# In-place transposed exponentials, a V product in three parts, early pair inputs and late weight sums in a fused attention and MLP kernel

## The chip, the cores and the metric

The kernel runs on one core of one Trainium2 chip. The metric is the device time of one execution in microseconds. The five engines work at once, each through its own instructions in order: PE (TensorE) multiplies matrices into PSUM, DVE (VectorE) and POOL (GpSimd) work element by element, ACT (ScalarE) applies functions and rounds, SP (SyncE) issues the transfers. Data lies in SBUF (128 partitions), sums of products in PSUM, the rest in device memory.

## What is computed

Attention with rotary positions over 4 batches of 8 heads, 576 tokens, 64 per head; its output, with the heads side by side, goes through a layer norm and a two-layer MLP with a residual sum. The weights are given in float64.

```python
scores = scale * np.matmul(q_rot, k_rot.transpose(0, 1, 3, 2))
scores = scores - np.max(scores, axis=-1, keepdims=True)
attn = np.exp(scores)
attn = attn / (np.sum(attn, axis=-1, keepdims=True) + 1e-09)
x = np.matmul(attn, v)                            # then (4, 576, 512)
xn = (x - mu) / np.sqrt(var + 1e-06) * g_ln
ch = np.maximum(xn @ w_ch1, 0.0) @ w_ch2          # 512 -> 2048 -> 512
return (x + ch).astype(np.float32)
```

## The kernel before

**First part.** The 32 heads are done as 16 head pairs, one after another (`attention(i)`). For each, PE makes scores in nine units of 128 by 576 (L430, the last one L426), each in one of four PSUM slots `sc` of two banks. DVE takes the maximum of each unit (L465), ACT the exponential with its row sums (L475), into a tile `p` (ring of two, each for two units; `p9` for the ninth). DVE transposes each unit in blocks of 32 from `p` into `pt` (L491, L488), of which there is one buffer for all nine units. When all nine are turned, PE multiplies them with V (`pv`, L539: 144 products of float32, 288 in the trace since each takes two passes) into two `sc` slots, DVE scales the result into `xt` (L555, L559) with inverse sums that went through memory (`write` L510, `read` L517 and L518). POOL rotates Q and K (L389, L391).

Between these lies other work: 32 weight tiles are decoded from float64 to float32 (`decode`, DVE L702 and L708, POOL L705, ACT L696 and L699) and split into a rounded high part and a low rest (`high` L721, `low` L725); the first 512 tokens (block 0) are normalised and go through the MLP as 32 units of 12 products (`mlp_unit`, L820). `weight_sums` makes, for each of eight stages (y, g), four sums of quarters of the weights (`tt` L771), splits them (L778, L781) and writes them to memory (L794) for the second part. A task of kind `how = {"POOL": 1.3, "DVE": 0.68}` goes to whichever of the two engines the planner finds free.

**Second part.** The other four blocks of 448 tokens are done as two pairs of blocks with a Strassen-like scheme: per pair eight stages of seven products of 12 matmuls (L973), with weights loaded from memory into a ring `w` of six buffers (`load_w`, L743 for the sums, L746 for plain quarters). `pair_inputs` makes the operands `x` of a pair: it loads four tiles of the normalised blocks for c = 0 into the one buffer `xc` of ring `ln` (L930), takes differences on POOL or DVE (L918), rounds on ACT and takes low parts (L900, L907), and then does the same for c = 1. The loads of the first pair wait for `late1`, that is, for all decoding, all weight sums and nearly all of block 0's MLP; the products of the second part use PSUM and SBUF that attention gives back (`late`, `switch`).

**Order.** Each piece of work is a task with a duration, dependencies, rings it takes from and gives to, and a priority. `Plan.run` runs the program once in its own time and records the tasks in the order in which they start there; that order is fixed on every engine. Priorities come from nominal times.

Of the kernel before, what the change touches and what calls it, by code (L numbers as in the profile page):

```python
# [10 lines left out]
F32 = mybir.dt.float32  # L11
# [9 lines left out]
P = 128  # L21
S = 576
# [19 lines left out]
RINGS = {"sc": 4, "m": 0, "p": 2, "p9": 1, "pt": 1, "x": 2, "xs": 3, "v": 1, "inv": 2, "w64": 2, "fw": 2, "w": 6, "h": 4, "xn": 1, "ln": 1, "sq": 1, "xt": 5, "n": 0, "o": 0, "tmp": 0, "ws": 2}  # L42
NPLAIN = 1
WP = 448
LATE = {"n": 6, "o": 13, "tmp": 9}
# [12 lines left out]
SLACK = 0.7  # L58
XPRIO = 1e4
XB = 0.0  # L60
WARM = 16
HOLD = {28: (14, 2), 29: (15, 0), 30: (15, 2), 31: (15, 4)}
ORDERED = True
ORDER = []
SIZES = 0.5, 2.0, 5.0, 12.0, 30.0
SHARE = 0.08, 0.01, 0.1, 0.3, 0.3
# [4 lines left out]
def mixed(x):  # L71
    for m in (0x7FEB352D, 0x846CA68B):
        x = ((x ^ x >> (16 if m == 0x7FEB352D else 15)) * m) & 0xFFFFFFFF
    return x ^ x >> 16


def chance(seed, i):
    return mixed((mixed(seed) + i * 0x9E3779B9) & 0xFFFFFFFF) / 2.0**32


def reorder(tasks):
    kinds = {}
    kind = [kinds.setdefault(t.fn.__code__, len(kinds)) for t in tasks]
    n = len(tasks)
    for seed in ORDER:
        m = mixed(seed)
        size, mode, later = SIZES[m % 5], m // 5 % 5, m // 25 % 5 == 0
        lo = int(chance(seed, 7) * n) if mode == 3 else 0
        for i in range(lo, min(lo + 60, n) if mode == 3 else n):
            t = tasks[i]  # L90
            if later and "SP" not in t.how:
                continue
            k = kind[i] + 1000003 if mode in (0, 4) else i
            if chance(seed, 2 * k + 100) < SHARE[mode]:
                d = size * (2 * chance(seed, 2 * k + 101) - 1)
                if later:
                    t.release += d
                else:
                    t.prio += d
# [10 lines left out]
class Plan:  # L110
# [32 lines left out]
    def run(self):  # L143
# [6 lines left out]
        while waiting:  # L150
            later = []
            started = False
            for t in waiting:
# [23 lines left out]
                e = min(t.how, key=lambda e: (begin(e), t.how[e]))  # L177
# [33 lines left out]
def rope_attention_then_ln_mlp(  # L211
# [32 lines left out]
    ap, xp, vpool, pp, ptp, smp = passing("attn"), passing("x", RINGS["x"]), passing("v", RINGS["v"]), passing("p", RINGS["p"]), passing("pt"), passing("small", 4)  # L244
# [27 lines left out]
    sums_w = {(y, g, i): dp.tile([P, 2, NC * P], F32, name=f"s{y}{g}{i}") for y in range(2) for g in range(4) for i in (3, 5, 6, 7)}  # L272
    split_w = {u: dp.tile([P, 2, NC * P], F32, name=f"v{u}") for u in UNITS}
# [158 lines left out]
    def attention(i):  # L432
# [3 lines left out]
        for c in range(5):  # L436
# [15 lines left out]
            ts = add({"PE": 0.6 if halved else 1.15 if c < 4 else 0.97}, go, need, N, take=["sc"] * len(units), give=["xk", "xq"] if c == 4 else [], lag=0.2, release=N - 2 if slow else 0, name=f"s{i}.{c}", behind=attention_order[-1:])  # L452
# [7 lines left out]
            for j, n in enumerate(units):  # L460
# [6 lines left out]
                def e(c=c, j=j, n=n):  # L467
                    if c == 4:
                        p = st["p", i, c] = pp.tile([P, S], F32, name="p9", bufs=1)
                    else:  # L470
                        if j == 0:
                            st["p", i, c] = pp.tile([P, 2, S], F32, name="p")
# [5 lines left out]
                take = ["p9"] if n == 8 else ["p"] if j == 0 else []  # L478
# [3 lines left out]
        for c in range(5):  # L482
            def turn(c=c):
                if ("pt", i) not in st:
                    st["pt", i] = ptp.tile([P, 9, S], F32, name="pt")
                pt, p = st["pt", i], st.pop(("p", i, c))
                if c == 4:
                    DVE.transpose(pt[:, 4], p)  # L488
                    return
# [5 lines left out]
            turned.append(add({"DVE": 0.68 if c == 4 else 1.36}, turn, need + turned[:1], N, take=["pt"] if c == 0 else [], give=["p9"] if c == 4 else ["p"], name=f"t{i}.{c}"))  # L495
# [30 lines left out]
        def pv():  # L526
            pt, v = st.pop(("pt", i)), st["v", i]
            st["pv", i] = tiles = [banks[k] for k in plan.task.got["sc"]]
            for b in range(18):
# [34 lines left out]
        t = add({"PE": 5.2}, pv, turned + [ev["v", i]], N, take=["sc", "sc"], give=["pt", "v"], lag=0.2, name=f"pv{i}")  # L564
        found = pieces(b)
        for piece in found:
# [10 lines left out]
            x = add({"DVE": dur}, go, [t, rd], N, behind=[] if fresh else [ev["fresh", n]], take=["xt"] if fresh else [], give=["sc", "sc", "inv"] if piece == found[-1] else [], of=t)  # L577
# [96 lines left out]
    def decode(k):  # L674
# [42 lines left out]
        t5 = add({"DVE": 0.68}, d2, [t4], prio, give=["w64"], port=True)  # L717
# [41 lines left out]
    def weight_sums(y, g):  # L759
# [3 lines left out]
        z, made = {}, {}  # L763

        def view(n):
            r, c = divmod(n, 2)
            f = st["fw", b].bitcast(F32).rearrange("p (r h) (c n) -> p r h c n", r=2, c=2)
            return f[:, r, :, c, :]
# [7 lines left out]
        def high(n):  # L776
            z[n] = wsp.tile([P, 2, NC * P], F32R, name="ws")
            ACT.copy(part(n, 0), view(n))  # L778
# [4 lines left out]
        how = {"POOL": 1.3, "DVE": 0.68}  # L783
        l = [t for k in range(k0, k0 + NC) for t in ev["wr", k]]
# [5 lines left out]
        for i, n, s in ((5, 3, s1), (7, 2, s3), (6, 0, s2), (3, 1, s4)):  # L790
            h = add({"ACT": 0.62}, lambda n=n: high(n), [s], prio, take=["ws"], behind=ev.get("sh", []))
            ev["sh"] = [h]
            read.append(add(how, lambda n=n: low(n), [h], prio, port=True))
            done.append(add({"SP": 512 / RATE}, lambda i=i, n=n: SP.dma_start(sums_w[y, g, i], raw(z[n])), read[-1:], prio, give=["ws"]))  # L794
        add({"NONE": 0.0}, lambda: None, read, prio, give=["fw"])
        ev["sums", (y, g)] = add({"NONE": 0.0}, lambda: None, done, prio)


    def mlp_unit(k, prev):
# [6 lines left out]
        dur = max(0.115, 0.008 + 0.43e-3 * W)  # L806
# [23 lines left out]
        if n and y % 8 != 4 and y:  # L830

            a = t = add({"PE": 12 * dur}, lambda: (group(0), group(1)), need + rest + ev["wr", k], prio, behind=ahead, take=["sc"], give=give, lag=0.2, name=f"m{k}")
        else:
            a = add({"PE": 6 * dur}, lambda: group(0), need + ev["wr", k], prio, behind=ahead, take=["sc"], name=f"m{k}")
            t = add({"PE": 6 * dur}, lambda: group(1), [a] + rest, prio + 0.5, give=give, lag=0.2)
# [43 lines left out]
    def switch():  # L879
        early.close()  # L880
        for name, n in LATE.items():
            kw = {"space": PSUM} if name == "n" else {}
            late[name] = ctx.enter_context(tc.tile_pool(name="late_" + name, bufs=n, reuse_waits="tile", **kw))
        late["acc"] = ctx.enter_context(tc.tile_pool(name="late_acc", bufs=1, reuse_waits="tile"))
# [313 lines left out]
```

## Time and profile before

| | |
|---|---|
| median of 3 runs | 766.96 us (765.75 to 774.95) |
| profiled execution | 771.92 us, its span 770.1 us |
| last V product ends | 452.2 us |
| PE busy, all | 648.7 us (84%) |
| DVE busy, all | 559.1 us (73%) |
| POOL, ACT busy, all | 439.1 us, 320.5 us |
| granted PE clock, mean | 0.902 |

Times in rows are microseconds from the start of the span, durations of one instruction ns. An engine's busy time is what its instructions cover; a row that gives a wait says how long the engine was idle before an instruction and what ended that.

### The profile page before, as it was taken

How to read it: one execution, taken by the hardware profiler on the slowest of the kernel's cores; microseconds unless marked ns; L12 is line 12 of the kernel's file. 1: busy time of each engine (PE TensorE's matmuls, PEld its weight loads, DVE VectorE, ACT ScalarE, POOL GpSimd, SP SyncE). 2: the span in 40 equal slices, each digit the busy share in tenths (PEclk: the TensorE clock that was granted, in tenths of full speed). 3: DMA queues.
4: the chain of work that ended last, by engine and by line, in shares of the span. 5: the costliest groups of instructions: out<-in, count | busy, mean ns of one | idle time of the engine just before them, and what ended most of it. 6: DMA issues, size and time to landing. Idle time of an engine off the chain costs nothing.

```text
span 770.1 us, 17931 instructions
## 1 busy us (share of the span) xinstructions
PE 648.7 (84%) x7218; PEld 512.7 (67%) x7218; DVE 559.1 (73%) x900; ACT 320.5 (42%) x662; POOL 439.1 (57%) x335
## 2 busy tenths in 40 slices
PE   6587677999878887877778644999999799999997
PEld 5464355676555564654556434788999699999997
DVE  5687876987778887786788435787676848757574
ACT  2355336625538356345555213534243305332230
POOL 3745765576677568687675015184166944544163
PEclk8878977899799998997999686999999899999999
DMA  9467775658796887767789632575876587666664
GB/s 263 128 192 200 187 216 193 180 151 265 175 269 219 261 246 273 193 210 256 204 253 307 205 106 76 176 254 184 292 214 220 190 261 250 213 219 215 218 201 145
DMA packets 92611, 163.33 MB, mean 212 GB/s; under 512 B 12144, under 2 KB 57712, under 8 KB 92528
## 3 DMA queue, kind: packets, MB, share of 16 engines
q1 hardware_dynamic: 91392, 161.33, 68.1%
q8 instruction: 57, 0.93, 0.5%
q10 hardware_dynamic: 1136, 0.85, 0.4%
q14 instruction: 26, 0.21, 0.1%
HBM read 124.32 MB, written 37.82 MB: 211 GB/s over the span
## 4 chain that ended last, share of the span: by engine, by line
PE 68%; DVE 15%; issue 5%; DMA 4%; ACT 4%; SPq 2%; POOL 1%; DVEq 0%; ACTq 0%; POOLq 0%
PE n L973 35%; PE sc L539 12%; PE sc L820 11%; PE sc L430 6%; DVE pt L491 5%; DVE mx L465 4%; ACT p L475 3%; PE sc L426 2%; DMA inv<-sums 2%; PE sc L617 1%; DMA xc<-hat 1%; POOL xc L918 1%; DVE xc L624 1%; DVE xt L555 1%; DVE fw L708 1%
## 5 line engine op out<-in xcount | busy, mean ns | idle before, releaser
L973 PE MATMUL n<-x,w 128*128 128x448 f32 x672 | 145.8, 375 | 17.8 <-ACT x L900 16.9
L475 ACT ACTIVATE p<-sc,mx 128x576 f32<-128x576 f32 x144 | 105.5, 738 | 126.7 <-DVE mx L465 119.4
L973 PEld LDWEIGHTS n<-x,w 128*128 128x128 f32 x672 | 127.9, 192 | 33.1 <-ACT x L900 18.2
L430 PE MATMUL sc<-xk,xq 64*128 64x288 f32 x512 | 109.2, 502 | 33.5 <-ACT p L475 20.7
L973 PE MATMUL n<-o,w 128*128 128x448 f32 x576 | 123.2, 372 | 4.6 <-DVE o L907 3.3
L539 PE MATMUL sc<-pt,v 32*64 32x160 f32 (+1 forms) x4608 | 100.5, 312 | 30.5 <-issue 24.1
L491 DVE STREAM_TRANSPOSE pt<-p 128x576 f32<-128x576 f32 x128 | 91.2, 752 | 41.7 <-PE sc L539 40.9
L973 PEld LDWEIGHTS n<-o,w 128*128 128x128 f32 x576 | 109.4, 191 | 16.3 <-DVE o L907 3.6
L539 PEld LDWEIGHTS sc<-pt,v 32*64 32x64 f32 x4608 | 89.0, 140 | 43.8 <-issue 29.1
L465 DVE TENSOR_REDUCE mx<-sc 128x1 f32<-128x576 f32 x144 | 101.3, 741 | 15.5 <-PE sc L430 13.3
L430 PEld LDWEIGHTS sc<-xk,xq 64*128 64x128 f32 x512 | 63.2, 219 | 71.7 <-ACT p L475 32.0
L900 ACT ACTIVATE o<-tmp 128x448 fp32r<-128x448 f32 x96 | 55.1, 578 | 100.4 <-PE n L973 46.0
L907 POOL TENSOR_TENSOR o<-tmp,o 128x448 fp32r<-128x448 f32 x57 | 72.4, 1298 | 25.2 <-ACT o L900 25.2
L1045 DVE TENSOR_TENSOR xt<-xt,n 128x448 f32<-128x448 f32 x80 | 49.0, 617 | 26.6 <-PE n L973 26.4
L725 POOL TENSOR_TENSOR w<-fw,w 128x512 fp32r<-128x512 f32 x26 | 33.2, 1280 | 56.1 <-ACT w L721 47.8
L705 POOL TENSOR_TENSOR fw<-fw,w 128x512 int32<-128x512 int32 x32 | 42.2, 1323 | 34.1 <-DVE fw L702 15.2
L820 PE MATMUL sc<-hh,w 128*128 128x512 f32 x128 | 49.5, 448 | 9.9 <-ACT p L475 9.9
L820 PE MATMUL sc<-xh,w 128*128 128x512 f32 x128 | 49.3, 452 | 5.7 <-ACT p L475 5.7
L1032 POOL TENSOR_TENSOR tmp<-tmp 128x448 f32<-128x448 f32 x16 | 21.4, 1336 | 55.3 <-DVE tmp L1011 55.3
L391 POOL TENSOR_TENSOR xs<-xs,rope_sb 128x576 f32<-128x576 f32 x30 | 46.7, 1556 | 0.5 <-DMA xs<-in_qk 0.5
L918 POOL TENSOR_TENSOR xc<-xc 128x448 f32<-128x448 f32 x16 | 21.4, 1334 | 41.8 <-DMA xc<-hat 38.3
L1011 DVE SCALAR_TENSOR_TENSOR tmp<-tmp 128x448 f32<-128x448 f32 x48 | 42.8, 912 | 0.2
(101 smaller groups left out, 972.7 us busy)
## 6 DMA issues: line engine op xcount, KB each, us to landing
w<-s SPq DMA_DIRECT2D x64, 512.0 KB
w<-v SPq DMA_DIRECT2D x96, 256.0 KB
v<-in_vp SPq DMA_DIRECT2D x64, 320.0 KB
s<-ws SPq DMA_DIRECT2D x32, 512.0 KB
xs<-in_qk SPq DMA_DIRECT2D x30, 288.0 KB
w<-in_w1p SPq DMA_DIRECT2D x16, 512.0 KB
v<-w SPq DMA_DIRECT2D x16, 512.0 KB
w<-in_w2p SPq DMA_DIRECT2D x16, 512.0 KB
```

Of the source, the lines that this page charges most:

```text
L391: eng().tensor_tensor(out=x[step], in0=x[step], in1=rope_sb[:, step], op=ALU.mult)
L430: PE.matmul(ps[:, a, :HS], lhsT=q[r, c * P : (c + 1) * P], rhs=k[r, KEYS[a]], start=True, stop=True)
L465: DVE.tensor_reduce(out=mx, in_=st["ps", i, n][:, :, :HS], axis=AX.XY, op=ALU.max, negate=True)
L475: ACT.activation(out=halves(p), in_=st.pop(("ps", i, n))[:, :, :HS], func=AF.Exp, bias=st.pop(("mx", i, n)), scale=1.0, accum_out=total)
L491: DVE.transpose(pt[:, 5 * j + c], p[:, j])
L539: PE.matmul(tiles[a // 2][j * D : (j + 1) * D, a % 2, x0 : x0 + (u1 - u0) * BLK], lhsT=v[r, of, k * P + j * D : k * P + (j + 1) * D], rhs= ...
L820: PE.matmul(ps, lhsT=wt, rhs=x, start=c + m == 0, stop=c + m == NC + 1)
L900: ACT.activation(out=o[0], in_=x(), func=AF.Relu if relu else AF.Copy)
L907: eng().tensor_tensor(out=lo, in0=x(), in1=raw(hi), op=ALU.subtract)
L973: PE.matmul(ps, lhsT=wt, rhs=x, start=fresh and kc + z == 0, stop=kc + z == 3, skip_group_check=True)
L1011: return lambda: DVE.scalar_tensor_tensor(out=out(), in0=x(), scalar=0.0, in1=y(), op0=ALU.max, op1=ALU.subtract)
L1045: DVE.tensor_tensor(out=o, in0=o, in1=ps(which, h), op=ALU.add)
```

## The change

Seven edits:

1. Exponentials are written straight into `pt`, of which there are now two buffers, and turned there in place, two units with one instruction; the rings `p` and `p9` are gone.
2. The V product is three tasks of 48 products each, between which others can be put.
3. `pair_inputs` loads both halves at once, into `xc`, three buffers of `sq` and one of `acc`, without waiting for `late1`, and takes the operands of both halves in turn.
4. For g = 3, `weight_sums` writes only the whole decoded weights to memory (`whole_w`, 1 MB each); `late_sums` reads them back in the second part (ring `lf`), makes the sums on POOL alone and writes them.
5. Rings: `w` 6 to 4, `inv` 2 to 1, `ws` 2 to 1, `sq` 1 to 3.
6. Every task's priority is a number from a table, and its earliest time is zero.
7. Planner durations, a few per cent each.

```diff
-RINGS = {"sc": 4, "m": 0, "p": 2, "p9": 1, "pt": 1, ..., "inv": 2, ..., "w": 6, ..., "sq": 1, ..., "ws": 2}
+RINGS = {"sc": 4, "m": 0, "pt": 2, ..., "inv": 1, ..., "w": 4, ..., "sq": 3, ..., "ws": 1, "lf": 0, "ls": 0}
+LATE = {"n": 6, "o": 13, "tmp": 9, "lf": 1, "ls": 1}
+DEFERRED = 6
+PLACES = (
+    "AAAFAGAPAUAKAFAAAZA-A)A;A8A#A#ArAvAzBFA^BQA[BdAeAAAoA[A}BMBVBGBcBdAwB8B6B(BoB%B:B,B[B=CBCRCFCmB~CPCeBnB=CVC1CuCvC&C=DYC:DDDgD%D!AjB7B.B_BACo",
...
+    places = "".join(PLACES)
+    for t, hi, lo in zip(tasks, places[::2], places[1::2], strict=True) if places else ():
+        t.prio, t.release = 0.1 * (len(CODE) * CODE.index(hi) + CODE.index(lo)), 0.0
...
-                        p = st["p", i, c][:, j]
+                    if n == 0:
+                        st["pt", i] = ptp.tile([P, 9, S], F32, name="pt")
+                    p = st["pt", i][:, 5 * j + c]
...
-                for j in range(2):
-                    DVE.transpose(pt[:, 5 * j + c], p[:, j])
+                p = st["pt", i][:, 4] if c == 4 else st["pt", i][:, c::5]
+                DVE.transpose(p, p)
...
-            for b in range(18):
+            for b in range(6 * part, 6 * part + 6):
...
-        t = add({"PE": 5.2}, pv, turned + [ev["v", i]], N, take=["sc", "sc"], give=["pt", "v"], lag=0.2, name=f"pv{i}")
+        t0 = t = add({"PE": 1.75}, lambda: pv(0), turned + [ev["v", i]], N, take=["sc", "sc"], name=f"pv{i}")
+        t = add({"PE": 1.75}, lambda: pv(1), [t], N)
+        t = add({"PE": 1.75}, lambda: pv(2), [t], N, give=["pt", "v"], lag=0.2)
...
+        if b < DEFERRED:
+            read, ev["sums", (y, g)] = make_sums(y, g, lambda: st["fw", b].bitcast(F32), l, prio, wsp, "ws", {"POOL": 1.3, "DVE": 0.68})
+            add({"NONE": 0.0}, lambda: None, read, prio, give=["fw"])
+            return
+        t = add({"SP": 1024 / RATE}, lambda: SP.dma_start(whole_w[y, g], st["fw", b].bitcast(F32)), [ev["d2", k] for k in range(k0, k0 + NC)], prio)
...
+    def late_sums(y, g, prio):
+        def load():
+            st["lf", y, g] = late["lf"].tile([P, NC, NC * P], F32, name="lf")
+            SP.dma_start(st["lf", y, g], whole_w[y, g])
+
+        t = add({"SP": 1024 / RATE}, load, [ev["whole", (y, g)], ev["late"]], prio, take=["lf"], name=f"lf{y}{g}")
+        read, ev["sums", (y, g)] = make_sums(y, g, lambda: st["lf", y, g], [t], prio, None, "ls", {"POOL": 1.3})
...
+                    if c == 0:
+                        if s == 0:
+                            x["all"] = lnp.tile([P, NC, BLOCK], F32, name="xc")
+                        x[c, s] = x["all"][:, s, :WP]
+                    elif s == 1:
+                        x[c, s] = lnp.tile([P, BLOCK], F32, name="acc")[:, :WP]
+                    else:
+                        x[c, s] = lnp.tile([P, BLOCK], F32, name="sq", bufs=RINGS["sq"])[:, :WP]
...
+                last = l[c, s] = add({"SP": 224 / RATE}, load, hats_, prio - 20, take=take, behind=[last] if last else [], name=f"hl{q}.{c}.{s}")
```

The table moves nearly every task. Three places show what matters below.

The first is DVE at the seam of the second and third head pair (`sc` are PSUM slots; `total` and `row` belong to the sums of a head pair, 208 before and 207 now to the second). Before, the third pair's first transpose is the last row shown, behind all of the second pair's:

```order
L491 STREAM_TRANSPOSE pt<-p 128x576 x2
L488 STREAM_TRANSPOSE pt<-p_622 128x576
L503 RECIPROCAL total_208<-total_208 128x9
L505 STREAM_TRANSPOSE row<-total_208 128x32
L465 TENSOR_REDUCE mx<-sc_111 128x1
L465 TENSOR_REDUCE mx<-sc_113 128x1
L465 TENSOR_REDUCE mx<-sc_114 128x1
L708 SCALAR_TENSOR_TENSOR fw<-w_269,fw 128x512
L725 TENSOR_TENSOR w<-fw,w 128x512
L702 TENSOR_SCALAR fw<-fw 128x512
L491 STREAM_TRANSPOSE pt<-p 128x576 x2
```

Now, at the same seam:

```order
L511 RECIPROCAL total_207<-total_207 128x9
L513 STREAM_TRANSPOSE row<-total_207 128x32
L499 STREAM_TRANSPOSE pt<-pt 128x576
L482 TENSOR_REDUCE mx<-sc_109 128x1
L482 TENSOR_REDUCE mx<-sc_110 128x1
L499 STREAM_TRANSPOSE pt<-pt 128x2x576
L482 TENSOR_REDUCE mx<-sc_111 128x1
L482 TENSOR_REDUCE mx<-sc_108 128x1
L499 STREAM_TRANSPOSE pt<-pt 128x2x576
L482 TENSOR_REDUCE mx<-sc_109 128x1
L482 TENSOR_REDUCE mx<-sc_111 128x1
L499 STREAM_TRANSPOSE pt<-pt 128x2x576 x2
```

What moved: the second pair's last two transposes stand among the third pair's maxima, and all five of the third pair's transposes stand on DVE ahead of the second pair's scaling; on PE the second pair's V product stands behind the third pair's last scores.

The second is PE at the end of attention. Before, the last V product is followed directly by the second part (`n`):

```order
L539 MATMUL sc_112<-pt,v 64x128
L539 MATMUL sc_112<-pt,v 64x160
L973 MATMUL n<-x_5343,w 128x448 x3
L973 MATMUL n<-x_5373,w 128x448 x3
```

Now three units of block 0's MLP, 36 products, stand between:

```order
L549 MATMUL sc_109<-pt,v 64x128
L549 MATMUL sc_109<-pt,v 64x160
L847 MATMUL sc_110<-hh,w 128x512
...
L847 MATMUL sc_108<-hl,w 128x512
L847 MATMUL sc_108<-hh,w 128x512
L1020 MATMUL n<-x_5143,w 128x448 x3
L1020 MATMUL n<-x_5141,w 128x448 x3
L1020 MATMUL n<-x_5143,w 128x448 x3
L1020 MATMUL n<-x_5141,w 128x448 x3
L1020 MATMUL n<-x_5222,w 128x448 x3
```

Over all 16 V products, nine stand uncut as 144 products in a row, seven are cut once, into 96 and 48, by four score products, by products of the MLP or by small ones of a layer norm.

The third is SP at the start of the second part. Before, the pair's input loads stand right behind the reads of the last inverse sums:

```order
L517 DMA inv<-sums_130 64x4x128
L518 DMA inv<-sums_130 64x64
L930 DMA xc<-hat_195 128x448 x2
L930 DMA xc<-hat_196 128x448 x2
L930 DMA xc<-hat_195 128x448 x2
L930 DMA xc<-hat_196 128x448 x2
L743 DMA w<-s_131 128x1024
```

Now the eight input loads (from `hat_194` and `hat_195`) stand two head pairs earlier, and behind the last stores of block 0 come weights and the late sums:

```order
L893 DMA out<-xt_559 128x512 x2
L755 DMA w<-s_131 128x1024
L787 DMA lf<-f_160 128x2048
L755 DMA w<-s_129 128x1024
L758 DMA w<-v_164 128x2x256
L758 DMA w<-v_165 128x2x256
L755 DMA w<-s_128 128x1024
L758 DMA w<-v_170 128x2x256
L758 DMA w<-v_171 128x2x256
L822 DMA s_141<-ls 128x1024
```

What moved: the transfers of `lf` (two) and `ls` (eight) are new on SP here, all within the first half of the first pair's products. On POOL the low parts and differences of the first pair stand ahead of the late sums, seven of them up to and with the low part of the second product's first operand. The weight sums left in the first part are now five of kind L771 and four of kind L781 on DVE.

## Rows read from the trace of the kernel before

**Rows 1.** Windows by stage: start:end, length, busy time per engine (instructions), PE clock, DMA share, GB/s.

```profile
0.00:452.20 452.20, 357.94 (x5790) 253.38 (x5790) 343.58 (x572) 216.74 (x475) 284.71 (x213) 0.86 0.72 217
452.20:496.60 44.40, 26.15 (x128) 20.25 (x128) 25.70 (x41) 17.01 (x30) 14.22 (x11) 0.77 0.39 119
496.60:606.50 109.90, 109.45 (x559) 98.36 (x559) 80.59 (x125) 41.20 (x76) 65.03 (x53) 1.00 0.74 237
606.50:612.20 5.70, 1.13 (x6) 0.44 (x4) 5.66 (x6) 3.36 (x6) 5.62 (x5) 0.76 0.47 137
612.20:770.10 157.90, 154.03 (x740) 140.27 (x740) 103.55 (x158) 42.15 (x75) 69.53 (x55) 0.99 0.67 210
```

**Rows 2.** Waits on DVE, 0 to 452.2: who waited for whom, us in total, times, longest.

```profile
DVE pt L491 <- PE sc L539: 40.9, 14, 9.3
DVE mx L465 <- PE sc L430: 13.3, 12, 6.6
```

**Rows 3.** Windows between the ends of V products, three of the sixteen (columns as in 1).

```profile
103.90:131.80 27.90, 21.61 (x355) 13.01 (x356) 18.72 (x32) 14.43 (x28) 16.46 (x13) 0.69 0.69 220
...
161.00:192.70 31.70, 30.59 (x408) 22.48 (x410) 25.50 (x42) 13.78 (x31) 20.27 (x16) 1.00 0.77 238
...
257.90:281.10 23.20, 19.51 (x354) 13.90 (x354) 21.10 (x35) 12.85 (x29) 11.92 (x10) 0.93 0.85 280
```

**Rows 4.** Lines of DVE by shape: names, shapes, xcount | busy us, mean ns | idle.

```profile
L491 DVE STREAM_TRANSPOSE pt<-p 128x576 f32<-128x576 f32 x128 | 91.2, 752 | 41.7 <-PE sc L539 40.9 <-ACT p L475 0.5
...
L771 DVE TENSOR_TENSOR fw<-fw 128x512 f32<-128x512 f32 x11 | 14.8, 1349 | 0.1
...
L781 DVE TENSOR_TENSOR ws<-fw,ws 128x512 fp32r<-128x512 f32 x8 | 9.6, 1212 | 0.2
...
L725 DVE TENSOR_TENSOR w<-fw,w 128x512 fp32r<-128x512 f32 x6 | 5.4, 902 | 3.4 <-ACT w L721 3.3
...
L505 DVE STREAM_TRANSPOSE row<-total 128x32 f32<-128x32 f32 x16 | 3.4, 212 | 0.6
```

**Rows 5.** Waits on PE from 0 to 452.2 (columns as in 2).

```profile
PE sc L539 <- issue: 24.1, 17, 5.3
PE sc L430 <- ACT p L475: 20.7, 14, 2.5
```

**Rows 6.** Page, DMA queues: the queue that fetches instructions (packets, MB, share).

```profile
q8 instruction: 57, 0.93, 0.5%
```

**Rows 7.** The chain of work, 440 to 500: start, us, what.

```profile
466.58 3.96 DMA xc<-hat
...
476.85 5.66 PE n L973 x20
482.50 0.77 PE sc L605 x2
...
486.18 0.40 PE sc L617 x8
...
495.69 0.88 PE sc L645 x8
```

**Rows 8.** The chain over the whole span: MLP units and pair products (columns as in 7).

```profile
271.43 3.00 PE sc L820 x12
...
612.17 154.07 PE n L973 x740
```

**Rows 9.** A window of dense traffic in the second part (columns as in 1).

```profile
536.60:556.60 20.00, 20.00 (x104) 18.44 (x103) 13.00 (x22) 3.36 (x6) 2.57 (x2) 1.00 0.86 285
```

**Rows 10.** The chain, 516 to 527: issue and landing of one weight load.

```profile
518.90 0.52 SPq L746
...
519.48 2.74 DMA w<-v
```

**Rows 11.** Lines of POOL by shape (columns as in 4).

```profile
L918 POOL TENSOR_TENSOR xc<-xc 128x448 f32<-128x448 f32 x16 | 21.4, 1334 | 41.8 <-DMA xc<-hat 38.3 <-DVE x L907 2.8
...
L907 POOL TENSOR_TENSOR x<-xc,x 128x448 fp32r<-128x448 f32 x12 | 14.5, 1226 | 8.1 <-ACT x L900 8.1
```

More of the change, by code (lines that the diff above doesn't have):

```diff
@@ L67 @@
 OVER = {"PE": 0.0, "DVE": 0.08, "ACT": 0.1, "POOL": 0.045, "NONE": 0.0}
 PORT = {"DVE": 0.13, "POOL": 0.05}
[L71 to L78, printed above, removed]
-def reorder(tasks):
[L82 to L99, printed above, removed]
+CODE = "ABCDEFGHIJKLMNOPQRSTUVWXYZabcdefghijklmnopqrstuvwxyz0123456789!#$%&()*+,-./:;<=>?@[]^_{|}~"
@@ L576, in attention @@
             dur = 2 * (0.14 + 0.067 * (c1 - c0)) * (c1 > c0) + 0.4 * tail
-            x = add({"DVE": dur}, go, [t, rd], N, behind=[] if fresh else [ev["fresh", n]], take=["xt"] if fresh else [], give=["sc", "sc", "inv"] if piece == found[-1] else [], of=t)
+            x = add({"DVE": dur}, go, [t, rd], N, behind=[] if fresh else [ev["fresh", n]], take=["xt"] if fresh else [], give=["sc", "sc", "inv"] if piece == found[-1] else [], of=t0)
             ev["x", i, n] = x
@@ L716, in decode @@
         t4 = add({"POOL": 1.3}, p1, [t2, t3], prio)
-        t5 = add({"DVE": 0.68}, d2, [t4], prio, give=["w64"], port=True)
+        t5 = ev["d2", k] = add({"DVE": 0.68}, d2, [t4], prio, give=["w64"], port=True)
         def high():
@@ L776, in high @@
         def high(n):
[L777 removed]
+            z[n] = (p or late["ls"]).tile([P, 2, NC * P], F32R, name=ring)
             ACT.copy(part(n, 0), view(n))
@@ L947, in pair_inputs, with at, diff, load @@
-        ev["x made"] = add({"NONE": 0.0}, lambda: None, made, prio)
+        x = {}
+        def at(c, s):
+            return lambda: x[c, s]
+        def diff(o, u, v):
+            return lambda: eng().tensor_tensor(out=o(), in0=u(), in1=v(), op=ALU.subtract)
+        two = {"POOL": 1.18, "DVE": BOTH}
+        l, hats_ = {}, [ev["hat", m, y2] for m in (a, b) for y2 in range(NC)]
+        last = None
+        for s in (0, 2, 3, 1):
+            for c in range(2):
+                def load(c=c, s=s):
+                    if c == 0:
[6 more added lines that the diff above has]
+                        x[c, s] = lnp.tile([P, BLOCK], F32, name="sq", bufs=RINGS["sq"])[:, :WP]
+                    SP.dma_start(x[c, s], hats[a if s < 2 else b][c + 2 * (s % 2)])
+                take = (["ln"] if c == 0 and s == 0 else []) + (["sq"] if c and s != 1 else [])
+                last = l[c, s] = add({"SP": 224 / RATE}, load, hats_, prio - 20, take=take, behind=[last] if last else [], name=f"hl{q}.{c}.{s}")
@@ new lines, in pair_inputs, with op @@
+        there = [ev["late1"]] if q == 0 else []
+        last = {0: [], 1: []}
+        def op(i, c, s, after):
+            t = operand((q, 0, c, i), at(c, s), after + there + ([ev["late"]] if i == 4 else []), prio, f"x{c}{i}")
+            last[c].append(t)
+            return t
+        l1 = [op(1, c, 0, [l[c, 0]]) for c in range(2)]
+        l3 = [op(3, c, 3, [l[c, 3]]) for c in range(2)]
+        t1 = [add(two, diff(at(c, 0), at(c, 2), at(c, 0)), [l1[c], l[c, 2]], prio, port=True) for c in range(2)]
@@ L949, in pair_stage @@
+        for c in range(2):
+            op(4, c, 1, [t4[c]])
+        ev["x made"] = add({"NONE": 0.0}, lambda: None, last[0] + last[1], prio, give=["ln"] + 3 * ["sq"])
     def pair_stage(q, m, y, g, k0, a, b):
```

144 lines of the change are left out of this document (80 added, 64 removed).

## Prediction, before the changed kernel had run

> **What bounds the kernel now.** I read the windows by stage first, then the waits of the engines inside the first stage, then the chain at the seam between the stages. The windows [rows 1] show a first part up to 452.2 us, when the last V product ends, a seam of 44.4 us in which PE is busy for 26.15 at a mean granted clock of 0.77, and a second part that PE fills: 109.45 of 109.9 us, then a hole of 5.7 us, then 154.03 of 157.9 us, all but the hole at 2.4 GHz. So nothing but the seam and the hole can be won behind 496.6 us; the rest is in the first part.
>
> There no engine is full: DVE is busy for 343.6 us of 452.2, PE for 357.9 at a clock of 0.86, POOL for 284.7. But between two V products DVE comes close, 21.10 of 23.20 us in the best interval shown, 25.50 of 31.70 and 18.72 of 27.90 in others [rows 3], and its longest wait is for one thing: 40.9 us in 14 waits, longest 9.3, by a transpose into `pt` for the V product that still reads it [rows 2]. With one `pt`, a head pair's V product and the next pair's transposes take turns. I take DVE as the engine that sets the first part's pace, with its other waits (108.6 idle less 40.9, that is 67.7 us) as its price of working with the rest.
>
> At the seam the chain [rows 7] goes through the pair's inputs: the second half's tiles are loaded only at 466.58, when the first half's operands have left the one buffer, and PE runs freely only from 476.85 on.
>
> **The first part, edit by edit.** *Two `pt` buffers:* the 40.9 us go. Not all are won: at the rows shown of DVE the next pair's transposes now stand ahead of the scaling, so what is late next is PE, which must make scores and V products closer together. PE was busy or without instructions ("issue") for 357.9 + 24.1 = 382 us [rows 1, 5], 84.5% of 452.2; the order takes 36 of 384 MLP products (9.0 us, below) out of this part. In 398 us, DVE's own sum below, PE would be at 373/398 = 94% at today's clock, and 90% if the clock rose to 0.90 (357.9 x 0.86/0.90 = 342, so 357 with both corrections). I let 5 us of the 40.9 come back for that; the bounds are 0 and all 40.9.
>
> *Turning in place:* 64 instructions replace 128. The 128 take 91.2 us of DVE, 712 ns of busy time each [rows 4]. A merged pair can save no more than the fixed part of one instruction, and that is below the 212 ns of a transpose of 32 columns [rows 4]: bounds 0 and 64 x 0.2 = 13 us. Instructions in a row already overlap (752 ns long, 712 apart), so I take a third, 0.07 us each, 4.5 us. Exponentials into `pt` instead of `p` cost ACT the same.
>
> *Late sums:* DVE had 11 + 8 of these operations, 14.8 + 9.6 = 24.4 us [rows 4]; the order leaves 5 + 4 in the first part, 5 x 1.349 + 4 x 1.212 = 11.6. That is 12.8 us less. Three more low parts of weights stand on DVE now (3 x 0.9 = 2.7 [rows 4]) and one more low part of block 0 (0.7 by the same row, less for its shape); sum +3.4. POOL loses six operations and is no bound. Two writes of 1 MB replace eight of 512 KB: 2.1 MB less traffic.
>
> *V product in three:* V products hold 17 waits for "issue", 24.1 us, longest 5.3 [rows 5], which no semaphore ends. An instruction queue fetched 0.93 MB in 57 packets, some 16 KB each [rows 6], and a V product is 288 matmuls and as many weight loads within 6 us: the pauses look like fetches, whose number the cuts don't change, and nine of 16 products stay uncut. I give the cuts 0; the bound is 7/16 x 24.1 = 10.5 us. The Trainium skill (Runtime: NRT & Kernel Launch, section Instruction fetch mechanics) says that the cost of crossing a 16 KiB block is mostly hidden. By that page the pauses would have another cause, which the cuts might remove, and the sum would be up to 10.5 lower; the trace bears it out only if the pauses are no fetches.
>
> *Smaller rings:* `ws` and `inv` with one buffer each add waits on ACT and SP. In the order the rounded sums stand many rows apart, so I take 0. The bound: 24 sums that each wait for the write before, at 3.3 us a transfer [rows 10], are 79 us on ACT, which is busy for only 216.7 of 452.2 us [rows 1], so it costs the path little.
>
> So DVE does 343.6 - 4.5 - 12.8 + 3.4 = 329.7 us of work, with 67.7 of waits 397.4, and 5 back: the last V product ends at **403 us** instead of 452.2. Bounds: at the best fill shown, 91%, 329.7/0.91 = 362; with the whole 40.9 back, 438.
>
> **From there to the end.** PE then has three MLP units, 3 x 3.00 = 9.0 us [rows 8]; the 1344 matmuls of the 112 pair products at 154.07/740 = 0.208 [rows 8], 279.8 us; the layer norms of the second pair's two blocks on PE, each 0.77 + 4 x 0.40 + 0.88 = 3.25 [rows 7], 6.5; and the end after PE, 157.9 - 154.03 = 3.9 [rows 1]. Together 299.2 us, against 770.1 - 452.2 = 317.9 now.
>
> *The seam:* inputs lie in SBUF two head pairs early, so the loads at 466.58 [rows 7] leave the path. What is late next are the operands: the second product waits for seven POOL operations, 4 x 1.226 + 3 x 1.334 = 8.9 us [rows 11], then a rounding. They start when the last weights are decoded and written out; the order puts that write of 1 MB inside the last V product, and at 285 GB/s [rows 9] it takes 3.7 us. The cover is 9.0 us of MLP units and 2.5 of the first pair product: I take 4 us of waiting, bounds 0 and 10.
>
> *The hole at 606.5:* 5.7 - 1.13 = 4.6 us [rows 1], with POOL busy 5.62 and DVE 5.66 of 5.70. The second pair's inputs now come a stage earlier; I take the hole as gone, bound 4.6.
>
> *Late sums' transfers:* two reads of 1 MB and eight writes of 512 KB fall into the first half of the pair products: 6.3 MB on top of 237 GB/s x 109.9 us = 26.0 MB [rows 1]. 32.3 MB at 285 GB/s, a dense window [rows 9], take 113.5 us: +3.6. That window was at 0.86 share, so 331 GB/s would be full: 0. At 250, which leaves gaps between transfers, +19. I take 4.
>
> *Four weight buffers:* a weight must land within three products, 3 x 12 x 0.208 = 7.5 us. One load took from 518.90 to 522.22, 3.3 us [rows 10]: covered, cost 0.
>
> Sum: 403 + 299.2 + 4 + 4 = 710.2 us of span. The profiled execution is 1.8 above its span and the median of the runs is 5.0 below that execution, so **707 us** for the median (the first part's end plus 304).
>
> **The rivals.** *PE takes DVE's place.* If PE can be filled to no more than 84.5%, as now, at a clock still at 0.86, 373/0.845 = 441 us for the first part, and the sum is 745. For it: of the intervals shown the one with the lowest clock, 0.69, is that in which DVE idles longest, 9.2 us [rows 3]; PE waits 20.7 us for exponentials to free its slots [rows 5]. Against: in the interval where PE was busy 30.59 of 31.70, the clock was 1.00 [rows 3], so denser work brings the clock back.
>
> *DVE packs better.* At 362 to 385 us the sum is 666 to 689. For it: two buffers loosen the lockstep that made other waits too. Against: scores, MLP and sums still cross between four slots.
>
> *The cuts cure PE's pauses.* 10.5 us off: 696. Against it stands that the count of instructions is the same.
>
> *Only the seam is won.* If the `pt` waits come back as waits for slots and inverse sums, 443 to 452, the sum is 747 to 756.
>
> *The weights starve PE (slower).* With four buffers a load that takes L from release to landing makes a product last (L + 2.5)/4. Over 112 products, to end above 782 each must lose 0.7 us, so L above 10.3 us, three times the row's 3.3. For it: `lf` of 1 MB and sums stand between weights on SP, in order, and wait there for POOL. Against: these are ten transfers among some 40 loads.
>
> *It does little.* 756 to 782, if the new order mostly misses the chip's timing.
>
> **Chances.** Forecast (first part 390 to 415, so 694 to 719): 0.45. The pauses cured: 0.06. Better packed: 0.17. PE in DVE's place, 719 to 745: 0.18. Only the seam: 0.07. Little: 0.04. Starved: 0.03. A measurement here tells about 2% from no change, so faster means below 751.6: 0.45 + 0.06 + 0.17 + 0.18 + half of 0.07 = 0.90; within 2%: 0.07; slower: 0.03. The range 674 to 746 leaves out the last three and a quarter of the better packed, 0.18.
>
> **What would show it.** Right: the wait of transposes for the V product gone or below 5 us; the last V product near 403; DVE's busy time up to there near 330; PE's pause between it and the pair products below 10 us and no pause for `hat` loads; "issue" in V products still near 24; the hole before the second pair gone; weights on SP waiting for PE, not PE for weights. Wrong: PE waiting tens of us for exponentials or DVE for scores with the clock still at 0.86, or matmuls of the second part at more than 0.21 us.

## The result, and the profile after

| | before | changed |
|---|---|---|
| median of four runs, us | 769.32 (765.75 to 774.95) | 706.12 (697.45 to 709.25) |
| span of the profiled execution | 770.1 | 695.3 |
| last V product ends at | 452.2 | 390.85 |
| from there to the end | 317.9 | 304.45 |

The ratio is 0.9135, with a 95% interval of 0.902 to 0.925. Ratios, here and below, are of mean times, and they leave out executions in a slower state of the chip (one of the changed kernel's four here, three of run 6's six), so that they need not agree with the medians. The profiled execution of the changed kernel is the fastest of its four; a second measurement on another chip (run 5 below) gave 701.37 us and 0.9057 (0.902 to 0.9095). The same kernel thus differs by 0.8% between two measurements, and a difference of that size between runs on two chips is not a finding by itself.

The windows by stage of the changed kernel, columns as in [rows 1]: the first part, the seam, the pair products.

```profile
0.00:390.85 390.85, 322.47 (x5755) 227.96 (x5755) 316.65 (x499) 210.73 (x467) 268.41 (x203) 0.93 0.80 238
390.85:408.00 17.15, 11.55 (x49) 8.96 (x49) 11.46 (x17) 6.88 (x14) 9.42 (x8) 0.99 0.91 328
408.00:695.30 287.30, 282.47 (x1415) 254.12 (x1415) 215.72 (x329) 98.67 (x181) 152.21 (x118) 0.99 0.76 240
```

Of the 74.8 us of span, 61.3 were won in the first part and 13.5 behind it. In the first part DVE works 26.9 us less and idles 74.2 us, where it idled 108.6; PE's mean granted clock is 0.93, where it was 0.86 [rows 1]. The waits of DVE in this part:

```profile
DVE xt L565 <- PE sc L549: 20.5, 6, 8.4
DVE mx L482 <- PE sc L447: 13.3, 13, 2.5
DVE pt L499 <- ACT pt L489: 7.5, 11, 1.7
...
DVE xt L569 <- PE sc L549: 5.3, 4, 3.2
```

The transposes wait for no V product any more (40.9 us in [rows 2]). What comes instead is the scaling (L565, L569), which waits 25.8 us for the V product's result. The waits of PE in the same stretch, to set beside [rows 5]:

```profile
PE sc L549 <- issue: 23.0, 14, 4.3
...
PE sc L443 <- ACT pt L489: 4.9, 6, 1.5
PE sc L447 <- ACT pt L489: 4.8, 7, 1.4
```

Scores wait for exponentials for 9.7 us; before, those of L430 alone waited 20.7 [rows 5]. The pauses for issue stand as they stood. DVE's lines that answer to [rows 4]:

```profile
L499 DVE STREAM_TRANSPOSE pt<-pt 128x1152 f32<-128x1152 f32 x64 | 87.0, 1364 | 7.6 <-ACT pt L489 7.5
...
L714 DVE TENSOR_SCALAR fw<-fw 128x512 uint32<-128x512 uint32 x32 | 17.1, 544 | 1.3 <-ACT fw L708 1.3
...
L737 DVE TENSOR_TENSOR w<-fw,w 128x512 fp32r<-128x512 f32 x9 | 9.3, 1029 | 3.1 <-ACT w L733 3.1
...
L811 DVE TENSOR_TENSOR ws<-fw,ws 128x512 fp32r<-128x512 f32 x4 | 3.7, 936 | 1.0 <-ACT ws L808 0.9
L801 DVE TENSOR_TENSOR fw<-fw 128x512 f32<-128x512 f32 x5 | 3.6, 722 | 0.0
```

PE's pauses behind the first part, by its timeline (start, us, what, idle before and what ended it):

```profile
400.07 2.68 PE L1020 MATMUL n<-x,w 128*128 128x448 f32 x12 [0.83 <-ACT x L928]
406.62 0.47 PE L1020 MATMUL n<-x,w 128*128 128x448 f32 x1 [3.87 <-ACT x L928]
408.01 18.60 PE L1020 MATMUL n<-x,w 128*128 128x448 f32 x83 [0.91 <-POOL x L935]
472.19 0.40 PE L629 MATMUL sc<-sq,mean_w 128*32 128x112 f32 x8 [0.68 <-DVE xc L636]
511.10 7.55 PE L1020 MATMUL n<-x,w 128*128 128x448 f32 x36 [0.31 <-DMA w<-s]
```

The seam costs PE 0.83 + 3.87 + 0.91 = 5.6 us, all for operands, none for a load; behind it PE waits 1.0 us to its end, and the hole ahead of the second pair [rows 1] is gone.

### The profile page after: what moved, and what is told of

It reads as the page before. It is cut to its first block, busy times and chain, and to the rows that moved or that the text cites. A ratio compares the mean times of both kernels' runs of the same rounds, so it can differ in the third digit from the quotient of the medians.

```text
span 695.3 us, 17868 instructions
## 1 busy us (share of the span) xinstructions
PE 616.5 (89%) x7218; PEld 491.0 (71%) x7218; DVE 543.8 (78%) x843; ACT 316.3 (45%) x662; POOL 430.0 (62%) x328
## 4 chain that ended last, share of the span: by engine, by line
PE 68%; DVE 14%; issue 7%; DMA 5%; ACT 3%; POOL 1%; SPq 1%; DVEq 0%; POOLq 0%; ACTq 0%
PE n L1020 38%; PE sc L549 12%; PE sc L847 10%; PE sc L447 6%; DVE mx L482 5%; DVE pt L499 3%; ACT pt L489 1%; DMA w<-in_w2p 1%; PE sc L443 1%; DVE xc L666 1%; DMA w<-s 1%; DMA w<-in_w1p 1%; PE sc L629 1%; DMA xs<-in_qk 1%; DVE fw L714 1%
## 5 line engine op out<-in xcount | busy, mean ns | idle before, releaser
L489 ACT ACTIVATE pt<-sc,mx 128x576 f32<-128x576 f32 x144 | 105.5, 738 | 120.7 <-DVE mx L482 117.4
L549 PE MATMUL sc<-pt,v 32*64 32x128 f32 (+1 forms) x4608 | 103.5, 312 | 26.7 <-issue 23.0
L1020 PEld LDWEIGHTS n<-o,w 128*128 128x128 f32 x576 | 107.9, 188 | 10.5 <-issue 0.2
L447 PE MATMUL sc<-xk,xq 64*128 64x288 f32 x512 | 95.6, 454 | 21.5 <-POOL xq L406 5.3
L482 DVE TENSOR_REDUCE mx<-sc 128x1 f32<-128x576 f32 x144 | 101.4, 742 | 16.0 <-PE sc L447 13.3
L499 DVE STREAM_TRANSPOSE pt<-pt 128x1152 f32<-128x1152 f32 (+1 forms) x80 | 98.1, 1241 | 7.6 <-ACT pt L489 7.5
L447 PEld LDWEIGHTS sc<-xk,xq 64*128 64x128 f32 x512 | 53.7, 196 | 57.1 <-ACT pt L489 16.6
L935 POOL TENSOR_TENSOR o<-tmp,o 128x448 fp32r<-128x448 f32 x44 | 57.8, 1326 | 38.4 <-ACT o L928 38.3
L1079 POOL TENSOR_TENSOR tmp<-tmp 128x448 f32<-128x448 f32 x16 | 20.7, 1291 | 47.6 <-DVE tmp L1058 47.6
L847 PE MATMUL sc<-xh,w 128*128 128x512 f32 x128 | 44.5, 409 | 2.8 <-ACT pt L489 2.8
L737 POOL TENSOR_TENSOR w<-fw,w 128x512 fp32r<-128x512 f32 x23 | 30.0, 1308 | 24.4 <-ACT w L733 24.3
L1058 DVE SCALAR_TENSOR_TENSOR tmp<-tmp 128x448 f32<-128x448 f32 x48 | 38.3, 806 | 0.4
L847 PEld LDWEIGHTS sc<-hh,w 128*128 128x128 f32 x128 | 25.5, 200 | 17.4 <-ACT w L733 5.0
```

The source lines that it names most:

```text
L447: PE.matmul(ps[:, a, :HS], lhsT=q[r, c * P : (c + 1) * P], rhs=k[r, KEYS[a]], start=True, stop=True)
L482: DVE.tensor_reduce(out=mx, in_=st["ps", i, n][:, :, :HS], axis=AX.XY, op=ALU.max, negate=True)
L499: DVE.transpose(p, p)
L549: PE.matmul(tiles[a // 2][j * D : (j + 1) * D, a % 2, x0 : x0 + (u1 - u0) * BLK], lhsT=v[r, of, k * P + j * D : k * P + (j + 1) * D], rhs= ...
L847: PE.matmul(ps, lhsT=wt, rhs=x, start=c + m == 0, stop=c + m == NC + 1)
L935: eng().tensor_tensor(out=lo, in0=x(), in1=raw(hi), op=ALU.subtract)
```

## Experiments

Ratios are to the kernel before on the same chip; "first part" is the end of the last V product in the profiled execution, "rest" the span behind it. Runs 1 to 4, 5 to 8 and 9 to 11 shared a chip; there the kernel before had medians of 775.21, 774.38 and 774.89 us. No profile of the kernel before was taken there, so its 452.2 and 317.9 us are from the first chip. In runs 1, 3, 7 and 9 the planner also keeps the pieces of a V product's scaling in their order, which the changed kernel does not.

| run | median us | ratio (95%) | first part | rest |
|---|---|---|---|---|
| 1 wait put back | 769.73 | 0.994 (0.9906 to 0.9973) | 467.8 | 301.1 |
| 2 no table | 764.11 | 0.9857 (0.9806 to 0.9909) | 442.2 | 319.3 |
| 3 places rounded | 731.96 | 0.9462 (0.94 to 0.9524) | 412.0 | 324.6 |
| 4 whole V, late | 715.65 | 0.9255 (0.9202 to 0.9307) | 403.8 | 306.6 |
| 5 changed, again | 701.37 | 0.9057 (0.902 to 0.9095) | 394.6 | 305.5 |
| 6 whole V, early | 722.4 | 0.9248 (0.9178 to 0.9317) | | |
| 7 sums early | 745.57 | 0.9636 (0.9582 to 0.969) | 412.4 | 335.9 |
| 8 seam alone | 773.07 | 0.9979 (0.9941 to 1.0017) | 466.0 | 307.9 |
| 9 new places | 720.22 | 0.9307 (0.9283 to 0.9331) | 405.3 | 308.6 |
| 10 five weights | 782.76 | 1.0087 (1.0057 to 1.0117) | 459.8 | 315.5 |
| 11 two transposes | 708.11 | 0.9133 (0.9098 to 0.9167) | 399.5 | 306.9 |

**Runs 1 to 3: the buffers, and the order.** Run 1 puts the wait back; the planner knows of it and orders the rest by the same table.

```diff
-            turned.append(add(..., turn, need, N, name=f"t{i}.{c}"))
+            turned.append(add(..., turn, need + turned[:1] + ([ev["pv", i - 1]] if c == 0 and i else []), N, ...))
+                    tc.add_manual_dep(list(traced)[n], st["pv done", i - 1], ..., reason="pt")
```

> The changed kernel with its places, in which the first transpose of a head pair waits once more for the last V product, as with one buffer. If the two buffers are what won (theory: the 40.9 us of DVE's waits of before), most of them come back: 25 to 41 us, so a median of 731 to 747, with DVE waiting for V products at the transposes for 25 us or more. If the places carry the gain (rival: the order of the tasks would also hide that wait), below 722. If it was DVE's smaller work (rival: 343.6 us before, 316.7 now), 700 to 712, since that work stays small.

The first part's window, and DVE's first waits in it (V products are L555 here, transposes L501):

```profile
0.00:467.80 467.80, 359.25 (x5784) 253.59 (x5784) 332.81 (x513) 213.28 (x473) 257.64 (x195) 0.84 0.69 205
```

```profile
DVE pt L501 <- PE sc L555: 54.0, 14, 6.9
DVE mx L482 <- PE sc L447: 18.3, 20, 2.7
```

Nearly all of the gain goes, more than expected, and with it the clock: 0.84. The places hide none of the wait, so the rival falls. DVE's work did not stay small, as the other rival had it: 332.8 us, 16 more than in the changed kernel. But the first part is 77 us longer than there, so that rival falls too.

```diff
-PLACES = ("AAAFAGAP...", ...)
+PLACES = ()
```

> The changed kernel without the table: every task keeps the place that the code gives it, as in the kernel before; buffers, merged transposes, late sums, cuts and early inputs stay. If the two buffers and DVE's smaller work are what won, the last V product ends at 400 to 420 us and the median is 706 to 735. If the table is what won (rival), the first part stays at 440 us or more and the median at 745 or more, with waits of DVE and PE in other places than the transposes.

The waits of DVE and PE in the first part (transposes L462, maxima L445, exponentials L452, scores L410, MLP L810):

```profile
DVE mx L445 <- PE sc L410: 34.5, 16, 8.6
DVE pt L462 <- ACT pt L452: 15.9, 20, 1.8
```

```profile
PE sc L810 <- ACT pt L452: 19.4, 13, 2.6
PE sc L410 <- ACT pt L452: 16.6, 16, 2.2
```

Without the table the transposes' wait for V products is gone, as forecast, but in its place DVE waits 34.5 us for scores (13.3 before [rows 2]) and its transposes 15.9 us for exponentials (0.5 before [rows 4]): together 36.6 us more, nearly the 40.9 that went. PE waits 36 us for exponentials to free its slots. That is no more than before, when it waited 20.7 us [rows 5] and the 15.6 of this line:

```profile
PE sc L820 <- ACT p L475: 15.6, 10, 3.4
```

The median and the end of the first part lie in the ranges that were set for the rival, the table. But run 1 has the table and gains next to nothing, so neither half stands alone: all edits but the table give 1.4%, all edits with the wait put back 0.6%, the whole change 9.4%. (What the other edits give with neither was not measured. The table was made for two buffers; that no order for one would do better isn't shown.)

```diff
-        t.prio, t.release = 0.1 * (...), 0.0
+        t.prio, t.release = 4 * round(0.1 * (...) / 4), 0.0
```

> The changed kernel with each place of the table rounded to whole steps of 4 us (ties then stand in the order of the code), nothing else. This says what a coarser order costs by itself. If the buffers won, a coarse order keeps most of it: median 700 to 720. If the fine order is what won (rival), 725 to 760.

The first part ends 17 us later than in run 5 and the rest is 19 us longer (in a profiled execution 6 us above the median), 4.5% by the ratios. DVE's longest wait is the scaling's for V products:

```profile
DVE xt L565 <- PE sc L549: 36.5, 12, 6.6
```

The median lies in the rival's range, 725 to 760: the fine order matters. Between "the buffers" and "the order" it is no either-or all the same, since a coarse order keeps over half of the gain.

**Runs 4 to 6: the cuts.** Run 4 keeps every engine's order but issues each V product whole, at the place of its last third; run 6 at that of its first.

```diff
-            for b in range(6 * part, 6 * part + 6):
+            for b in range(18) if part == 2 else ():      # run 6: part == 0
```

> The changed kernel in the same order on every engine, but each V product issued in one piece, at the place of its last third. The prediction gave the cuts 0: median within 5 us of the changed kernel, and 20 to 28 us of PE's waits for issue inside V products, as in both kernels so far (24.1 and 23.0). If the cuts keep PE from running ahead of its instructions (rival), the waits rise by 5 to 10.5 us and the median by 4 to 11.

> The changed kernel once more, beside the next three on one chip, so that a per cent between them can be read: 0.905 to 0.925 of the kernel before, by every theory.

> As the run with whole V products, but each issued at the place of its first third. If the loss there came from PE's pauses (rival), it comes back here, and issue waits go above 28 us. If it came from where V products end, 13 us later over the first part with DVE waiting 47.1 us for them in place of 25.8 (theory), that wait falls to 30 us or less here, and what stood between the thirds, scores and MLP products, comes later instead: DVE waits for scores rise above 13 us; the median lies within 5 us of the changed kernel.

PE's pauses for issue in the first part, and DVE's first two waits, of run 4:

```profile
PE sc L549 <- issue: 24.4, 16, 3.5
```

```profile
DVE xt L565 <- PE sc L549: 37.5, 10, 6.9
DVE xt L569 <- PE sc L549: 9.6, 3, 4.6
```

and the same of run 5, the changed kernel again:

```profile
PE sc L549 <- issue: 26.5, 16, 3.8
```

```profile
DVE xt L565 <- PE sc L549: 22.2, 7, 6.3
...
DVE xt L569 <- PE sc L549: 4.8, 3, 3.4
```

The pauses don't come from whole V products: 24.4 us without cuts, 26.5 with. Yet the cuts seem to be worth 1 to 2%: 0.9255 and 0.9248, against 0.9057 in run 5, on run 6's own chip, and 0.9135 in the first measurement. So both runs missed the 5 us (0.7%) that was expected. In run 4 the scaling waits 47.1 us for V products, 20 more than in run 5. Run 6 lies 2.1% above run 5, so a V product issued early doesn't help either; its profiled execution was 12 us longer than its median, and its waits are not read. That scores and MLP products have to pass between the thirds, lest DVE wait for one or the other, fits both runs; shown is only run 4's half of it.

**Run 7: the late sums.** The two late stages' sums are made where their weights were written out, in the one `ws` buffer; those writes and reads of 1 MB go.

```diff
-        t = add({"SP": 1024 / RATE}, load, [ev["whole", (y, g)], ev["late"]], ...)
-        read, ... = make_sums(..., [t], prio, None, "ls", {"POOL": 1.3})
+        read, ... = make_sums(y, g, lambda: st["fw", 2 * g + y]..., wsp, "ws", {"POOL": 1.3, "DVE": 0.68})
```

> The changed kernel with the two late stages' sums made in the first part again, right where the whole weights were written out; the rest of the table stands. Theory (by the prediction): DVE gets 6 + 4 more of those operations, 8 to 13 us, and the first part ends that much later, some of it hidden; the second part loses 4 us of transfers at most: median 4 to 12 us above the changed kernel, and more where the fine order is hurt (the rounded places cost some 20 us). Rival (POOL takes them, DVE's idle time hides them): within 3 us, or below.

The pair products' start on PE, and what ACT does ahead of it (lines of ACT from 412 to 452):

```profile
451.01 0.74 PE L1023 MATMUL n<-x,w 128*128 128x448 f32 x1 [26.15 <-ACT x L931]
```

```profile
L811 ACT CAST ws<-fw 128x512 fp32r<-128x512 f32 x7 | 4.3, 617 | 24.6 <-DMA s<-ws 24.6
```

44 us lost by the medians, nearly four times the top of the 4 to 12 that were expected: by the profiled executions 18 in the first part, though DVE is busy only 4.5 us longer there (321.4 against 316.9 in run 5), and 30 behind it, nearly all in one pause of 26.15 us. There the last sums go through one buffer, six of the seven waiting 3.4 to 5.8 us for the write before, and the pair's operands wait for them, as for all sums of the first part (`late1`).

**Runs 8 and 10: the seam.** Run 8 is the kernel before with the new `pair_inputs` (and `"sq": 3`, `"w": 5`); run 10 has `"w": 5` alone.

> The kernel before with only the pair inputs of the changed one (loaded tile by tile as the heads' tiles are written, five buffers in place of one; the weight ring has five buffers in place of six to make room). Theory: the first part stays at 452 us, give or take 5; the seam's pause of PE for the loads goes, and so does the hole before the second pair, 4.6 us: together 10 to 19 us, a median of 0.975 to 0.987 of the kernel before. Rival (the operands' POOL work or the last weights are what the seam waits for): 0.99 to 1.0.

> The kernel before with five weight buffers in place of six, nothing else, to read the run with the pair inputs alone, whose first part ended at 466 us. Theory: the ring does nothing, 0.995 to 1.005 of the kernel before, last V product at 452 to 458. Rival (the ring is what lengthened that run's first part): 1.008 to 1.02, last V product at 462 or later.

PE's pauses behind the first part in run 8, the last two at the old hole:

```profile
469.74 0.44 PE L993 MATMUL n<-x,w 128*128 128x448 f32 x1 [3.67 <-DVE xt L555]
470.72 3.82 PE L993 MATMUL n<-x,w 128*128 128x448 f32 x11 [0.54 <-DVE x L908]
477.02 0.74 PE L993 MATMUL n<-x,w 128*128 128x448 f32 x1 [2.49 <-ACT x L901]
...
613.34 0.56 PE L993 MATMUL n<-o,w 128*128 128x448 f32 x1 [2.37 <-ACT o L901]
616.61 15.78 PE L993 MATMUL n<-o,w 128*128 128x448 f32 x68 [2.71 <-POOL o L908]
```

Run 8 missed: 0.998 where 0.975 to 0.987 was expected; that is in the range of the rival, by which the seam waits for operands, and the pauses shown at the seam do end by operands and by DVE's scaling. Its rest is 307.9 us against 315.5 in run 10, so the early inputs are worth 7.6 us behind the first part; by the ratios, from two chips, it is 1.1% in all. In the profiled executions run 8's first part is 6.2 us longer than run 10's, but run 10's was its fastest by 5.7 us, so what the early inputs cost there is open. The five weight buffers that made room cost 0.9% by themselves, against the expectation too. And the hole stays: 2.37 + 2.71 us, ended by operands `o`, not by the second pair's inputs.

**Run 9: other places.** The durations that the planner reckons with were set by the trace, and the table made anew for them.

```diff
-            {"PE": 1.75}, lambda: pv(0) ...     {"DVE": ... else 1.34}, turn
+            {"PE": 2.2}, lambda: pv(0) ...      {"DVE": ... else 1.44}, turn
-PLACES = ("AAAFAGAP...", ...)
+PLACES = (another table)
```

> The changed kernel with another table of places, for which the durations that the planner reckons with were set by rows of the changed kernel's trace (a third of a V product 2.2 us with its share of the pauses, a merged transpose 1.44, a POOL addition 1.37, a rotation 1.5, a pair product's half 1.248), and the pieces of a V product's scaling kept in their order. If the order of the first part is worth what the rounded places lost (theory), an order made for the measured durations brings 5 to 15 us more: 686 to 697, with the last V product before 388. If run-to-run timing on the chip blurs such an order (rival): within 4 us of the changed kernel's 701, or above.

The rival's outcome: 2.8% slower than the changed kernel (0.9307 against 0.9057). PE's pauses in V products grew, to 37.0 us in the first part:

```profile
PE sc L549 <- issue: 37.0, 19, 3.2
```

That is 10.5 us more than in run 5, and the first part ends 10.7 us later; whether the one makes the other isn't shown. This order, fitted to mean durations, is not better on the chip; what makes the table of the change good there is left open. No run beat the changed kernel.

**Run 11: the merging.** The same order on every engine, each merged transpose split in two.

```diff
-                DVE.transpose(p, p)
+                for j in range(2):
+                    DVE.transpose(p[:, j], p[:, j])
```

> The changed kernel in the same order on every engine, with each merged transpose split again into two of 576 columns. The prediction gave the merging 4.5 us of DVE: transposes busy for 103 to 104 us in place of 99, and as much later an end of the first part, median 701 to 707. Bound: 13 us, 714. Rival (DVE's waits of 74 us swallow it): under 703.

```profile
L503 DVE STREAM_TRANSPOSE pt<-pt 128x576 f32<-128x576 f32 x128 | 90.8, 748 | 1.6 <-ACT pt L489 1.5
```

By this line of DVE, 90.8 us for the 128 against 87.0 for the 64: 3.8 us, and a first part that ends 4.9 us later than in run 5, 0.8% in all. The median, 708.11, is above the 703 below which the waits would have swallowed the work, so DVE's work seems to be on the path. That isn't shown beyond doubt: PE's pauses are 2.7 us longer than in run 5 too (29.2 against 26.5), and the changed kernel itself had 0.9135 on its first chip.

## Why the prediction was right, and where it wasn't

**Total.** 707 us were forecast and 706.12 measured, but part of this closeness is chance. The sum was 710.2 us of span and the profiled execution has 695.3 (run 5: 700.1): 12 us less in the first part (8 in run 5) and 2.7 (1.7) behind it. (The first part's terms add up to 402.4, not 403.) The conversion from span to median took 3.2 us off, since before's profiled execution was above its median; this one is 8.7 us below its own.

**The `pt` wait, right in size, incomplete in cause.** It is gone. DVE idles 74.2 us where 67.7 + 5 were forecast; inside that, 25.8 came back as waits for V products and the older waits fell to 48.4. So the total of the waits came out by two errors that cancel: too little for PE being late, and the older waits held constant at 67.7. The step credited the gain to the two buffers and let 5 us come back as if the order were given. Run 2 has the buffers and a first part 10 us below that of [rows 1]; run 1 has the order and saves nothing there. The price of the order should have been a term of its own.

**DVE's work: 316.65 us, forecast 329.7.** The step that failed is the price of the operations that collide with POOL. The sums that stayed cost 5 x 0.722 + 4 x 0.936 = 7.3 us where 11.6 was forecast with before's means, and the 32 shifts of the decoding (L714), which the sum didn't touch, fell from 26.8 to 17.1. Both means hold waits for POOL. Two lines of before's shift (the second has number: least, median, most ns), and one case on DVE and on POOL:

```profile
L702 DVE TENSOR_SCALAR fw<-fw 128x512 uint32<-128x512 uint32 x32 | 26.8, 851 | 1.8 <-ACT fw L696 1.8
```

```profile
L702 DVE TENSOR_SCALAR fw<-fw x32: 377/422/1642, 26.0 to 411.9; 128x512 uint32<-128x512 uint32 x32
```

```profile
186.82 1.64 DVE L702 TENSOR_SCALAR fw<-fw 128x512 uint32<-128x512 uint32 x1
```

```profile
186.31 1.87 POOL L391 TENSOR_TENSOR xs<-xs,rope_sb 128x576 f32<-128x576 f32 x1
```

The shift starts under POOL's operation and ends at 188.46, 0.28 us after that one's end at 188.18; its median is 0.42. All 15 long shifts of before (0.69 us and more) start under a running operation of POOL and end 0.28 us after one's end; none of the 17 others starts under one. The sums do the same: the eight of the 11 that took 1.06 us and more start under one and end 0.55 us after one's end. The Trainium skill (SBUF — State Buffer, section SBUF: two separate sides) calls the port pair that DVE and POOL share an exclusive lock that is held for the whole instruction; the trace agrees. Such a mean is a property of an order and of one execution's timing, not a price: the same five sums took 0.722 us on average in the changed kernel, 0.929 in run 5 and 1.198 in run 11, whose order is the same. The shifts also fell in runs 1 and 2 (means 574 and 594 ns), so the table alone is not why; which edit did it is open. Two smaller misses: three MLP sums moved behind the first part with their products (2.0 us, not counted), and three more low parts of weights cost 3.9 us for 2.7.

**Merged transposes**: 4.2 us less by the trace, 3.8 by run 11, 4.5 forecast.

**Cuts: the step failed.** They got 0 because PE's pauses would stay, and the pauses did stay. But by runs 4 and 6 the cuts are worth 1 to 2% in this order: their worth is not in PE's pauses. What the step never priced is what may pass between the thirds; run 4's longer waits for V products point to it. The rival "cures PE's pauses" fell.

**Smaller rings: 0 was right only through the late sums.** The bound named, sums that each wait for the write before, is what run 7 shows: 24.6 us of ACT waiting, on the path, as soon as the last eight sums fall at the end of the first part. So the small ring leans on the late sums; run 7 with two `ws` buffers was not tried.

**Behind the first part: 304.45 us, forecast 307.2.** MLP 8.41 us (9.0), the seam 5.6 (4), late transfers next to nothing (4): PE waited 0.31 us for a weight, once. By the chain of waits the pair matmuls ran at 180.52/876 = 0.206 us (0.208):

```profile
390.84 8.41 PE sc L847 x36
...
511.10 180.52 PE n L1020 x876
```

Four weight buffers cost PE nothing there, as forecast; SP waited for PE instead, by its two load lines:

```profile
SPq L758 <- PE n L1020: 84.5, 43, 8.7
SPq L755 <- PE n L1020: 70.7, 53, 2.6
```

But the step priced the ring for the second part alone. The first part's weights pass through it too, and run 10 lost 0.9% with one buffer less in the order of before; what four cost the first part of the changed kernel was not measured.

The gain behind the first part is the table's as well: run 2 has the early inputs and the late sums and a rest of 319.3 us. The hole went, but not for the reason given: runs 2 and 8 have the early inputs and keep 5 us of it, waiting for operands of the hidden layer (`o`). With the rounded table 2.4 us are left, with the unrounded one it is closed, in runs 1 and 7 too. The step had read what was busy in the hole, not what ended the waits, which before's timeline of PE names:

```profile
608.42 0.47 PE L973 MATMUL n<-o,w 128*128 128x448 f32 x1 [1.30 <-ACT o L900]
612.17 1.11 PE L973 MATMUL n<-o,w 128*128 128x448 f32 x2 [3.27 <-DVE o L907]
```

**Rivals.** PE didn't take DVE's place: 322.47 + 23.0 of 390.85 us is 88%, at a clock of 0.93, and exponentials hold scores back for under 10 us.

## What to carry to other kernels

A second buffer moves a wait elsewhere unless the order of the work is made to use the freedom; price the order as a term of its own, and expect the two not to add up (here 1.4% without the new order, 0.6% with it but with the wait put back, 9.4% with both). A mean duration that holds waits for another engine belongs to its order: use the median or the least, and price the collisions apart. For every pause that a sum removes, read which wait ends it, not what is busy in it.

## What the runs showed of the hardware

**The pauses "issue" in V products are instruction fetches.** One of the changed kernel, by PE's timeline:

```profile
362.74 0.86 PE L549 MATMUL sc<-pt,v 32*64 32x128 f32 x32
366.98 1.37 PE L549 MATMUL sc<-pt,v 32*64 32x160 f32 x36 [3.39 <-issue]
```

In the records of the trace a packet of 16 KB of the instruction queue starts at 364.6 and lands at 365.6, 1.4 us before the matmuls go on. So it is wherever, inside a V product of before (15 times) or after (16 times), more than 0.34 us pass from one matmul's start to the next one's, the first matmuls left aside: the last packet landed 1.1 to 1.6 us before the pause ended. Counted over PE's records (weight loads, matmuls, semaphores) in order of time, all 31 lie at record 193 or 194 modulo 256, whichever matmul of a V product that is (the 134th to the 279th). The count of packets fits: 57 [rows 6], and PE has 14,612 records, that is 57.1 times 256. In the changed kernel these pauses are all of the 23.0 us; in before they are 18.2 of the 24.1, and the longest, 5.3 us, stands at the start of the first V product, at no such place. The pauses belong to the place in the program: an order decides which of these places fall into V products, and cutting a V product doesn't remove them. The Trainium skill (Runtime: NRT & Kernel Launch, section Instruction fetch mechanics) calls the cost of such a block mostly hidden; here the traces differ, with 23.0 us of such pauses in a first part of 390.85 and 26.5 in run 5's of 394.6.
